# Two roundings moved behind attention steps, VectorE's w_out sums one down step later, six stores on ScalarE's queue

## The chip, the cores and the metric

One core of a Trainium2 chip runs the kernel. The metric is the device time of one execution in microseconds; of the kernel before there are three runs, 1019.55, 1022.45 and 1023.5, median 1022.45. Engines are called as the profile calls them: PE (TensorE; PEld its weight loads), DVE (VectorE), ACT (ScalarE), POOL (GpSimd), SP (SyncE, which here only issues DMAs).

## What is computed

A retention block, whose output is the input of a SwiGLU feed-forward block:

```python
scores = scale * np.matmul(q, k.transpose(0, 1, 3, 2))        # (8, 8, 576, 576), head_dim 64
Dmat = np.where(rel >= 0, gamma[:, None, None] ** rel, 0.0)   # rel = query position - key position
attn = np.matmul(scores * Dmat, v)
x = attn.transpose(0, 2, 1, 3).reshape(4608, 512)
g, val = x @ w_gate, x @ w_val                                # 512 -> 1536
out = (g * (1.0 / (1.0 + np.exp(-g))) * val) @ w_out          # 1536 -> 512
```

## The kernel before

**Attention.** Each of the 8 batches has 4 pairs of heads; pair i is one unit of work. `tick(t)` (L737) is attention step t: it finishes pair t-2, multiplies pair t-1 and prepares pair t, so that three pairs are in flight. On PE a step is own values (L532), new states (L543), earlier values (L555, L559) and scores (L567, L573). Around them ACT copies the even states (L584), scales the keys (`keys`, L507) and the queries (L489), and copies outputs into x (L626, L656); DVE masks the scores (L580, L590), sums states (L596 to L608) and transposes queries and keys of the next pair (L492). `load(i)` (L254) issues a pair's loads on SP: four for q and four for k of 128-byte rows, one each for k and v as rows.

**Feed-forward.** The 4608 tokens are cut into tiles: one of 512, then four of 1024. Tile 0 is multiplied plainly: `up0(f)` (L842) makes the gate and value products of hidden block f, f = 0 to 11, into two of the four PSUM banks; ACT takes the silu (L856), DVE multiplies by it (L857). Then `down0(f)` (L862) multiplies the twelve hidden blocks by w_out in the order of `down_order` (8, 9, 1, 3, 10, 4, 6, 11, 5, 7, 0, 2), each into all four banks, so the first down step needs the banks of the last up step back. The later tiles use a fast matrix multiplication, with sums of x blocks, weight blocks and hidden blocks as operands (`up_stage`, `down_step`, L1042, L1186, L1381).

**Rounding of weights.** Weights arrive as raw float32 in 18 pieces (`order`), each of two halves, 36 halves j. For half j, `split(j)` takes it apart on ACT (L389, L390) and `rounding(j)` puts it together on DVE (L406, L407) and then calls `split(j + 1)`. The last piece, m = 17, is the last sixth of w_out; its halves are j = 34, needed by `down0(10)`, and j = 35, needed by `down0(11)`. In the kernel before, the plan of the up steps calls both just ahead of the last one, `up0(11)`.

**Sums of w_out.** The later tiles need sums of w_out blocks, 26 operands that are stored to DRAM (`dn_ops`). `out_sums(last)` (L919) makes them in nine groups of up to three operands: `groups` are the sums of the first two thirds of w_out on POOL, `last_groups` those of the last third on DVE. Sums are L879, L881 and L886; each operand's store (L956) is issued on SP as soon as the group is written down, so SP's queue meets the stores in the order of the program and waits at each for its sum. The sums rotate through a few places in SBUF (seven for POOL): a place is free again when its store has landed. `negate` (L915, L917) writes two negated blocks on ACT that POOL's sums read.

**The order around the change** is written out by hand; each engine executes its instructions in the order of the program. The up steps 2 to 11 of tile 0 come from a list, `plan`, that mixes `up0`, roundings, loads and steps 4 to 9 (`tick_at`); step 9 follows `up0(11)`. Then the loop over the twelve down steps (counted from 0) runs `down0`, step 10, 11, 12 and 13 after down steps 1, 3, 6 and 8, and after each down step one group of DVE's sums and one of POOL's. `go_on(n)` issues the next n pieces of an attention step that are still held back. After down step 9, `early_sums` starts the sums of x and of the up weights for tile 1 on DVE and POOL (L1042).

DMAs of SP and ACT count on eight semaphores, taken in turn as the build lays them out; an instruction that issues a DMA waits until the one that had its semaphore before has landed.

Of the kernel before, what the change touches and what calls it, by code (L numbers as in the profile page):

```python
# [131 lines left out]
def kernel(  # L132
# [32 lines left out]
    nc = tc.nc  # L165
# [15 lines left out]
    NQ = NF // 4  # L181
# [54 lines left out]
    def needed(n):  # L236

        last = (min(starts[n] + TW, NT) - 1) // S
        return last * HP + HP - 1 + 3
# [112 lines left out]
    order = [0, 1, 2, 3, 4, 5, 6, 12, 7, 8, 13, 9, 10, 14, 11, 15, 16, 17]  # L352
# [27 lines left out]
    def split(j):  # L380

        i, f = halves[j]
        bits = bits_of(i, f)
        top, ulp = [rest[:, part_at + 512 * (2 * n + j % 2) : part_at + 512 * (2 * n + j % 2 + 1)] for n in range(2)]
        blocks = lambda a: a.rearrange("p (c m) -> p c m", m=P)
        nc.scalar.activation(out=blocks(top), in_=bits[:, :, :, 1].bitcast(F32), func=AF.Prelu, scale=2.0 ** -112, alpha=2.0 ** 32)  # L389
        nc.scalar.activation(out=blocks(ulp.bitcast(I32)), in_=bits[:, :, :, 0].bitcast(U32), func=AF.Copy, scale=2.0 ** -29)  # L390
        parts[j] = top.bitcast(I32), ulp.bitcast(I32)
        m = j - 2 if 1 < j < 4 else j // 2
        if f and m != RAWS and m + RAWS + (m < RAWS) < len(order):
            if j == 3:
                held.append(lambda: load_w(m + RAWS + (m < RAWS)))
            else:
                load_w(m + RAWS + (m < RAWS))

    def rounding(j, ahead=True):

        i, f = halves[j]
        dst = weights[i][1][f].bitcast(I32)
        top, ulp = parts.pop(j)
        nc.vector.tensor_scalar(out=dst, in0=top, scalar1=3, scalar2=None, op0=ALU.logical_shift_left)  # L406
        nc.vector.tensor_tensor(out=dst, in0=dst, in1=ulp, op=ALU.add)  # L407
        if ahead and j + 1 < len(halves):
            split(j + 1)
# [289 lines left out]
    ends = [(n, x, hl) for n in range(2) for x in range(2) for hl in range(2)]  # L699
# [28 lines left out]
    pieces = []  # L728
# [95 lines left out]
    def go_on(n):  # L824
        for _ in range(min(n, len(pieces))):
            while part_on():
                pass

    def part_on():

        if pieces and isinstance(pieces[0], list):
            pieces[0].pop(0)()
            if pieces[0]:
                return True
            pieces.pop(0)
        elif pieces:
            pieces.pop(0)()
        return False
# [23 lines left out]
    def down0(f):  # L862
        for i, bank in enumerate(banks):
            nc.tensor.matmul(bank, hid0[f][:, ts(i, P)], w_dn[:, f // 4, f % 4].rearrange("p d x -> p (d x)"),
                             start=(f == down_order[0]), stop=(f == down_order[-1]))
# [10 lines left out]
    def add(eng, op, view, to=None):  # L876
        dst, srcs = view(int(op[1])) if to is None else to, [view(int(a)) for a in op[2:]]
        if op[0] == "neg":
            eng.tensor_scalar(out=dst, in0=srcs[0], scalar1=-1.0, scalar2=None, op0=ALU.mult)  # L879
        elif op[0] == "nad" and eng is nc.vector:  # L880
            eng.scalar_tensor_tensor(out=dst, in0=srcs[0], scalar=-1.0, in1=srcs[1], op0=ALU.mult, op1=ALU.subtract)  # L881
        elif op[0] == "nad":
            eng.tensor_tensor(out=dst, in0=srcs[0], in1=srcs[1], op=ALU.add)
            eng.tensor_scalar(out=dst, in0=dst, scalar1=-1.0, scalar2=None, op0=ALU.mult)
        else:
            eng.tensor_tensor(out=dst, in0=srcs[0], in1=srcs[1], op=ALU.add if op[0] == "add" else ALU.subtract)  # L886

    up_sets = [[dr.tile([P, 1792], F32, name=f"up{qd}_{o}") for o in SETS] for qd in range(NQ)]
    dn_ops = [dr.tile([P, 768], F32, name=f"dn{i}") for i in range(N)]
# [9 lines left out]
    def events_of(text):  # L899
        r = []  # L900
        for line in text:
            i, s = line.split("|")
            slot, ops = s.split(":")
            r += [(int(op[1]), op) for op in terms(ops)] + [(None, int(slot), int(i))]
        return r
# [10 lines left out]
        for n, s in enumerate((3, 5)):  # L916
            nc.scalar.mul(out=negatives[n], in_=w_dn[:, 0:2, s // 2, s % 2], mul=-1.0)  # L917

    def out_sums(last):  # L919


        place = {}

        def free(p):
            if not any(p is q for q in x0_places):
                sum_places.append(p)

        qs = NQ - 1 if last else slice(0, NQ - 1)
        eng, sum_places = (nc.vector, vector_places) if last else (nc.gpsimd, pool_places)
        events = events_of(OUT_SUMS if last else signed)  # L930

        def view(s):
            if s > 13:
                return negatives[s - 14]
            return w_dn[:, qs, s // 2, s % 2] if s < 8 else place[s]

        def used(e):
            return [e[1]] if e[0] is None else [int(a) for a in e[1][2:]]

        def release(k):  # L940

            for s in list(place):
                for e in events[k + 1 :]:
                    if s in used(e):
                        break
                    if s == e[0]:
                        free(place.pop(s))
                        break
                else:
                    free(place.pop(s))  # L950

        def do(k):
            e = events[k]
            if e[0] is None:
                _, slot, i = e
                nc.sync.dma_start(out=dn_ops[i].rearrange("p (q x) -> p q x", q=NQ)[:, qs], in_=view(slot))  # L956
            else:
                new = sum_places.pop(0)
                add(eng, e[1], view, new)
                if e[0] in place:  # L960
                    free(place[e[0]])
                place[e[0]] = new
            release(k)

        r, ends = [], [k for k, e in enumerate(events) if e[0] is None]
        for g in range(0, N, 3):
            lo, hi = ends[g - 1] + 1 if g else 0, ends[min(g + 2, N - 1)] + 1

            def group(lo=lo, hi=hi):
                for k in range(lo, hi):  # L970
                    do(k)

            r.append(group)
        return r
# [151 lines left out]
    def early_sums():  # L1126

        x_outer, x_inner, *_ = x_sets(1)
        _, _, w_outer, w_inner, store = w_sets(0)
        p = [w_inner(2) + store(2, True), w_outer(5), x_inner(2, nc.gpsimd), w_outer(6), w_inner(6) + store(6, True), x_inner(6, nc.gpsimd)]  # L1130
        v = [f for o in (5, 6, 3, 7) for f in x_outer(o, nc.vector)]
        return p, v
# [309 lines left out]
    def next_load(t):  # L1442
        if t + AHEAD < NP:
            load(t + AHEAD)

    groups, last_groups = out_sums(False), out_sums(True)
    todo = [m for m in range(3, len(order))]
    plan = []

    def round_until(i):  # L1450
        while todo and order.index(i) >= todo[0]:
            m = todo.pop(0)
            plan.extend(lambda j=j: rounding(j) for j in (2 * m, 2 * m + 1))
# [2 lines left out]
    plan.insert(1, lambda: tick(HP, HP, FIRST))  # L1456
    tick_at = {2: 4, 3: 5, 5: 6, 7: 7, 10: 8, 11: 9}
    for f in range(2, NF):
        round_until({4: 12, 6: 13, 8: 14, 9: 15, 10: 16, 11: 17}.get(f, f + 2))
        if f + 1 == NF:  # L1460
            plan.append(lambda: pool_places.extend(wide_places))
            plan.append(negate)
        plan.append(lambda f=f: up0(f, range(HP)))
        if f - 1 in tick_at and f < 7:
            plan.append(lambda t=tick_at[f - 1]: next_load(t))
        if f in tick_at and f > 2:
            plan.append(lambda t=tick_at[f]: tick(t, HP, FIRST))
            if tick_at[f] == HP + 1:
                plan.append(end_transposes)
        if f in (7, 10):  # L1470
            if f == 10:
                plan.append(lambda: next_load(9))
            plan.append(lambda t=tick_at[f]: next_load(t))
    assert not todo
    for f in plan:
        f()
    tick_at = {1: 10, 3: 11, 6: 12, 8: 13}
    for m, f in enumerate(down_order):
        down0(f)
        go_on(6)  # L1480
        if m in tick_at:
            tick(tick_at[m], HP, FIRST, tick_at[m] + 1 < needed(1))
            go_on(2)
        if last_groups:
            last_groups.pop(0)()
        if groups:
            groups.pop(0)()
        if m == 9:
            early, early_x = early_sums()
            go_on(len(pieces))  # L1490
        if m >= 9:
            for f in early_x[:4]:
                f()
            del early_x[:4]
            for f in [f for fs in early[:2] for f in fs]:
                f()
            del early[:2]
# [62 lines left out]
```

## Time and profile before

| what | value |
|---|---|
| median of 3 runs | 1022.45 us |
| profiled execution: time | 1022.88 us |
| profiled execution: span | 1021.2 us |
| granted PE clock, mean | 0.998 |
| PE busy | 1003.4 us (98%) |
| DVE busy | 718.9 us (70%) |
| POOL busy | 555.6 us (54%) |
| ACT busy | 286.2 us (28%) |

The attention of the first pairs and the loading of weights fill the first 60 us. Tile 0's up steps end at about 119 us, its down steps at 176 us; tile 1 runs to about 400 us, and the rest is shared by the other three. Times in the views count from the start of the span. A timeline row has the start, the time it covers, engine, line, operation, the tile written and the tile read, the shape and a count; in square brackets, how long the engine was idle before it and what released it. In a row of waits there are the total, the count and the longest. The table of stretches has the busy time of PE, PEld, DVE, ACT and POOL, the granted clock, the DMA engines' busy share and GB/s. Engine names that end in q are the engine's own queue, which issues DMAs.

### The profile page before, as it was taken

Reading aid. Unit: us, or ns where it says so; the run is one execution under the profiler, and the core shown is the slowest. Engines: PE = TensorE matmul, PEld = TensorE weight load, DVE = VectorE, ACT = ScalarE, POOL = GpSimd, SP = SyncE. Lnnn points to the kernel's source line nnn. Section 1 sums busy time; section 2 is a strip of 40 time slices with the busy share of each in tenths; the row PEclk is TensorE's granted clock in tenths of the full one; section 3 lists DMA queues with packets and bytes.
Section 4 is the critical chain, followed back from the end, with each engine's and each line's share of the span. In section 5 each row is a group of like instructions: output and inputs, shape, how many; then the busy total and the mean of one; then the engine's idle time right before and its main releaser. Section 6 shows DMA issues by size and latency. Waiting matters only on the chain.

```text
span 1021.2 us, 21316 instructions
## 1 busy us (share of the span) xinstructions
PE 1003.4 (98%) x8336; PEld 823.2 (81%) x8336; DVE 718.9 (70%) x1215; ACT 286.2 (28%) x636; POOL 555.6 (54%) x579
## 2 busy tenths in 40 slices
PE   6999999999999999999999999999999999999998
PEld 5645455888888888888888888888888888888887
DVE  5478889678787766876688678848575767566644
ACT  4466522132423312133332101233320012232110
POOL 3400348979572218575565248756672586566515
PEclk9999999999999999999999999999999999999999
DMA  9999877777496888746658776434454454445652
GB/s 239 256 273 258 198 213 257 204 232 207 124 262 162 247 205 229 200 158 189 188 167 226 191 187 202 166 127 148 168 179 148 146 194 145 144 156 179 186 158 96
DMA packets 278892, 194.38 MB, mean 190 GB/s; under 512 B 212552, under 2 KB 246088, under 8 KB 278792
## 3 DMA queue, kind: packets, MB, share of 16 engines
q1 hardware_dynamic: 251464, 94.70, 36.4%
q10 hardware_dynamic: 26688, 97.92, 29.0%
q8 instruction: 66, 1.08, 0.5%
q0 software_dynamic: 640, 0.39, 0.2%
q14 instruction: 34, 0.28, 0.1%
HBM read 154.04 MB, written 38.93 MB: 189 GB/s over the span
## 4 chain that ended last, share of the span: by engine, by line
PE 86%; DMA 5%; DVE 4%; ACT 2%; issue 1%; SPq 1%; POOL 0%; ACTq 0%; DVEq 0%
PE bankC L1186 11%; PE bankB L1186 11%; PE bankA L1186 11%; PE bankE L1186 11%; PE bankB L1381 7%; PE bankE L1381 7%; PE bankC L1381 7%; PE bankA L1381 6%; PE outer L1186 2%; PE inner L1186 2%; PE outer L532 2%; DMA rest<-in_moe_w_out_dram 2%; PE inner L573 1%; PE inner L543 1%; PE outer L559 1%
## 5 line engine op out<-in xcount | busy, mean ns | idle before, releaser
L1042 POOL TENSOR_TENSOR rest<-rest 128x512 f32<-128x512 f32 (+1 forms) x141 | 150.5, 1079 | 156.2 <-DVE rest L1042 114.1
L1201 POOL TENSOR_TENSOR arena<-rest,io 128x256 f32<-128x256 f32 x156 | 114.6, 746 | 82.7 <-ACT io L1200 82.3
L1200 ACT ACTIVATE io<-rest 128x256 f32<-128x256 f32 x192 | 79.3, 417 | 208.4 <-DVE rest L1042 146.1
L1186 PE MATMUL bankB<-rest,arena 128*128 128x256 f32 x448 | 114.9, 381 | 0.2
L1042 DVE TENSOR_TENSOR rest<-bankB,rest 128x512 f32<-128x512 f32 x116 | 78.3, 683 | 48.4 <-PE bankB L1186 33.8
L1186 PE MATMUL bankC<-rest,arena 128*128 128x256 f32 x416 | 106.3, 380 | 0.2
L1186 PE MATMUL bankA<-rest,arena 128*128 128x256 f32 x412 | 105.3, 380 | 0.6 <-DVE rest L1042 0.4
L1042 DVE TENSOR_TENSOR rest<-bankA,rest 128x512 f32<-128x512 f32 x110 | 74.3, 683 | 39.9 <-PE bankA L1186 19.7
L1042 DVE TENSOR_TENSOR rest<-bankC,rest 128x512 f32<-128x512 f32 x110 | 74.6, 684 | 33.7 <-PE bankC L1186 18.0
L1186 PE MATMUL bankE<-rest,arena 128*128 128x256 f32 x372 | 95.0, 381 | 0.4 <-DVE rest L1042 0.3
L1186 PEld LDWEIGHTS bankB<-rest,arena 128*128 128x128 f32 x448 | 84.5, 190 | 13.0 <-DVE rest L1042 1.5
L1042 DVE TENSOR_TENSOR rest<-bankE,rest 128x512 f32<-128x512 f32 x106 | 71.7, 684 | 30.3 <-PE bankE L1186 12.6
L1186 PEld LDWEIGHTS bankC<-rest,arena 128*128 128x128 f32 x416 | 78.3, 190 | 12.2 <-DVE rest L1042 1.0
L1186 PEld LDWEIGHTS bankA<-rest,arena 128*128 128x128 f32 x412 | 77.9, 190 | 12.3 <-DVE rest L1042 1.8
L1186 PEld LDWEIGHTS bankE<-rest,arena 128*128 128x128 f32 x372 | 69.8, 190 | 11.9 <-DVE rest L1042 1.8
L1042 POOL TENSOR_TENSOR arena<-arena 128x256 f32<-128x256 f32 (+1 forms) x76 | 70.9, 957 | 8.5 <-DMA up<-arena 4.8
L886 POOL TENSOR_TENSOR rest<-rest 128x512 f32<-128x512 f32 x21 | 29.1, 1407 | 77.8 <-DVE rest L407 59.3
L1381 PE MATMUL bankB<-arena 128*128 128x256 f32 x264 | 61.0, 381 | 0.0
L1381 PE MATMUL bankE<-arena 128*128 128x256 f32 x264 | 60.8, 380 | 0.0
L886 POOL TENSOR_TENSOR arena<-arena 128x768 f32<-128x768 f32 x24 | 47.1, 1964 | 15.5 <-DVE arena L1201 14.9
L1381 PEld LDWEIGHTS bankE<-arena 128*128 128x128 f32 x264 | 50.0, 190 | 6.9
L1381 PEld LDWEIGHTS bankB<-arena 128*128 128x128 f32 x264 | 49.8, 190 | 6.9
(267 smaller groups left out, 1891.6 us busy)
## 6 DMA issues: line engine op xcount, KB each, us to landing
arena<-up ACTq DMA_DIRECT2D x63, 896.0 KB, 4.6
arena<-dn ACTq DMA_DIRECT2D x65, 384.0 KB, 3.7
arena<-dn SPq DMA_DIRECT2D x39, 384.0 KB, 3.2
out_dram<-rest SPq DMA_DIRECT2D x31, 256.0 KB, 3.0
qk<-in_q_dram SPq DMA_DIRECT2D x108, 72.0 KB, 3.6
qk<-in_k_dram SPq DMA_DIRECT2D x108, 72.0 KB, 4.0
dn<-rest SPq DMA_DIRECT2D x26, 256.0 KB, 3.2
up<-arena SPq DMA_DIRECT2D x13, 512.0 KB, 4.0
```

The costliest lines, as they stand in the source:

```text
L532: m = nc.tensor.matmul(value(i, hl, c), s["v"][rows, at], ret[rows, c % 2 if whole(i) else hl, c // 2], start=start, stop=start, skip_grou ...
L543: nc.tensor.matmul(z[half[hl], r, c], s["kn"][chunk(i, hl, 2 * c + r)], s["v"][rows, at], start=True, stop=True, skip_group_check=True)
L559: nc.tensor.matmul(xr[half[hl]] if c + 1 == NC else value(i, hl, c), state[half[hl], c, :], s["qT"][half[hl], ts(c, L)], start=False, stop ...
L573: nc.tensor.matmul(sc[chunk(i, hl, 2 * c + r)[0], r if whole(i) else hl, c], kT[half[hl], at], qT[half[hl], at], start=True, stop=True, sk ...
L886: eng.tensor_tensor(out=dst, in0=srcs[0], in1=srcs[1], op=ALU.add if op[0] == "add" else ALU.subtract)
L1042: eng.tensor_tensor(out=out, in0=a, in1=b, op=ALU.add if sign > 0 else ALU.subtract)
L1186: m = nc.tensor.matmul(b[:, g * TB : (g + 1) * TB], w[:, g], x, start=(opens and g == 0), stop=True, skip_group_check=True)
L1200: nc.scalar.activation(out=s, in_=src[:, 0:TB], func=AF.Silu)
L1201: (nc.vector if busy and o != 2 else nc.gpsimd).tensor_tensor(out=hid[:, qd, 2 * H + h, 2 * T + t], in0=src[:, TB : 2 * TB], in1=s, op=ALU ...
L1381: nc.tensor.matmul(b[:, m * TB : (m + 1) * TB], lhs[:, qd, ts(m, P)], w[:, qd], start=(opens and qd == 0 and m == 0), stop=(qd == NQ - 1), ...
```

## The change

The roundings of the last piece, j = 34 and j = 35, leave the plan ahead of `up0(11)`. Half 34 is rounded at the end of the plan, behind step 9; half 35 in down step 1, behind all pieces of step 10, which are now issued at once there. DVE's groups of w_out sums begin in down step 1 instead of 0. POOL's begin with two groups in down step 0 and go on with one in each. The first six stores of POOL's sums, those of its first two groups, are issued on ACT's queue instead of SP's.

```diff
-    def out_sums(last):
+    def out_sums(last, soon=0):
...
-                nc.sync.dma_start(out=dn_ops[i].rearrange("p (q x) -> p q x", q=NQ)[:, qs], in_=view(slot))
+                queue = nc.scalar if k in ends[:soon] else nc.sync
+                queue.dma_start(out=dn_ops[i].rearrange("p (q x) -> p q x", q=NQ)[:, qs], in_=view(slot))
...
-    groups, last_groups = out_sums(False), out_sums(True)
+    groups, last_groups = out_sums(False, 6), out_sums(True)
...
     for f in range(2, NF):
-        round_until({4: 12, 6: 13, 8: 14, 9: 15, 10: 16, 11: 17}.get(f, f + 2))
+        round_until({4: 12, 6: 13, 8: 14, 9: 15, 10: 16, 11: 16}.get(f, f + 2))
...
-    assert not todo
+    assert todo.pop() == len(order) - 1 and not todo
+    plan.append(lambda: rounding(2 * len(order) - 2))
     for f in plan:
         f()
...
             tick(tick_at[m], HP, FIRST, tick_at[m] + 1 < needed(1))
-            go_on(2)
-        if last_groups:
+            go_on(2 if m > 1 else len(pieces))
+        if m == 1:
+            rounding(2 * len(order) - 1)
+        if last_groups and m:
             last_groups.pop(0)()
-        if groups:
+        for _ in range(min(len(groups), 1 if m else 2)):
             groups.pop(0)()
```

## The prediction

> **What bounds the kernel now.** I read the page's busy shares first, then the waits of TensorE (PE), then timelines of the stretch that the change touches, 112 to 260 us.
>
> ```profile
> PE 1003.4 (98%) x8336; PEld 823.2 (81%) x8336; DVE 718.9 (70%) x1215; ACT 286.2 (28%) x636; POOL 555.6 (54%) x579
> ```
>
> PE is idle for 17.8 us of 1021.2: 7.7 in the first 20 us, which the change leaves alone, and after 60 us crumbs of 0.5 and less, but for one. The waits of PE between 112 and 260 us have one row:
>
> ```profile
> PE bankE L864 <- DVE arena L857: 1.9, 1, 1.9
> ```
>
> So the change can win there and nowhere else. VectorE's (DVE) timeline shows who made it late: the last two roundings (L406, L407) stand ahead of the product L857 that frees bankE. The table of stretches shows what followed: PEclk, the granted clock, is 0.62 in the 4.5 us after the stall and 1.00 elsewhere.
>
> ```profile
> 120.91 1.64 DVE L407 CUSTOM_DVE_ANT_0 rest<-rest 128x1024 uint16<-128x1024 uint16 x1
> 122.47 1.49 DVE L406 TENSOR_SCALAR rest<-rest 128x512 int32<-128x512 int32 x1
> 124.10 1.53 DVE L407 CUSTOM_DVE_ANT_0 rest<-rest 128x1024 uint16<-128x1024 uint16 x1
> 125.55 0.68 DVE L857 TENSOR_TENSOR arena<-bankE,io 128x512 f32<-128x512 f32 x1
> ```
>
> ```profile
> 124.40:126.30 1.90, 0.02 (x1) 0.02 (x1) 1.90 (x4) 0.00 (x0) 1.90 (x2) 1.00 0.96 210
> 126.30:130.80 4.50, 4.50 (x7) 1.94 (x8) 4.32 (x13) 0.00 (x0) 0.45 (x1) 0.62 0.88 156
> ```
>
> **The stall goes.** In the new order L857 follows step nine's key transpose, which ends at 120.51. Its silu (ACT L856) starts at 118.30 and moves earlier, since the last split leaves the place ahead of it. So L857 runs 120.5 to 121.2; PE wants bankE at 124.38. The margin of 3.2 us is the cover; the stall returns only if L857 slips by more. That removes 1.90 us of stall. The three pairs of products behind it took 1.42, 1.71 and 1.41 us where every other pair takes 0.86: 4.54 - 2.58 = 1.96 us of half clock. Together **3.86 us**. Check: from the first product of the step to the next attention step PE needs 10.93 us here (121.54 to 132.47) and 7.06 one step later (134.73 to 141.79); the difference is 3.87. Every later date of PE is its row less 3.86.
>
> [...]
>
> **The moved roundings.** Each is an L406 and an L407, 0.42 and 0.69 us alone (99.35 and 99.91), 1.42 to 1.6 beside POOL's sums. The first now follows step nine's transposes (ends about 126.7), where DVE waits until 131 for step ten's scores anyway: hidden, 1 to 3 us into a gap of 4. Its weight is due in down step 4 (counted from 0), near 140. The second follows step ten's transposes and is due in down step 7, near 153; the cover is some 12 us, but the w_out sums queue behind it.
>
> **ScalarE's six stores.** ACT's scaling of step nine ends at 123.82; the split moved there (two of 0.57) ends at 125.0. Six issues of 0.4 to 0.5 us follow (SP's rows of the same store: 0.39 to 0.46, one 1.03), to 128. The POOL sums they store are ready: started at 116.8, once L917 is 1.1 us earlier, five sums of 1.3 to 1.7 end at 124. ACT is next needed at 131.1 for step ten's copy (134.93 - 3.86), so the issues cost nothing there; the cover is 3 us.
>
> But they reach SP's queue. All these DMAs share eight semaphores, and the built program has SP's v load of pair 11 wait for the first store's landing, the q loads of pair 10 for the second, third and fourth, its k loads for the fifth and sixth. Before, SP ran unhindered:
>
> ```profile
> 124.08 0.58 SPq L287 DMA_DIRECT2D v<-in_v_dram x1
> 124.77 3.42 SPq L282 DMA_DIRECT2D qk<-in_q_dram x4
> 128.23 2.12 SPq L282 DMA_DIRECT2D qk<-in_k_dram x4
> 130.45 0.44 SPq L287 DMA_DIRECT2D kn<-in_k_dram x1
> 130.99 0.59 SPq L287 DMA_DIRECT2D v<-in_v_dram x1
> 132.86 3.39 SPq L956 DMA_DIRECT2D dn<-rest x6
> ```
>
> A store of this size lands 2.3 to 4.7 us after its issue. I take 2.7 (172.48 to 175.23 in the trace, with little beside it): v at 127.8 instead of 124.08, the q and k loads 128.4 to 132.8, kn at 132.9 instead of 130.45, landing 3.6 later (4.1 in the row of 123.54, which stood behind a load of q and k) at 136.5, v at 137.8. Step eleven on PE needs kn scaled and v by 138.2 (142.07 - 3.86) and the transposed keys by 139.5 (143.37 - 3.86). ACT scales kn (0.96) and qk (0.87), DVE transposes (1.43): 136.5 + 3.3 = 139.8. **A new wait of 0.3 us**; between 0, at a landing of 2.3, and 6, at 4.7 with kn as late as its first use allows (130.45 to 137.66).
>
> **DVE's sums, a step later.** Behind those transposes (139.8) stand the second rounding (1.1), the first two groups (seven ops, 2.4: POOL waits then), step ten's masks and states (2.75), to 146.05; four sums of about 1.2 beside POOL (147.38 to 150.96 had three in 3.58), the transposes of step eleven (to 151.7, wanted at 152.6), six more sums (7.2), and step eleven's masks and states, done at 161.6. PE wants those at 161.2: **0.4 us** (0 to 1.5). PE is then 3.86 - 0.3 - 0.4 = 3.16 ahead.
>
> **POOL sets how much of this stays.**
>
> ```profile
> 138.12 1.35 POOL L886 TENSOR_TENSOR rest<-rest 128x512 f32<-128x512 f32 x1 [11.36 <-DMA dn<-rest]
> ...
> 161.32 5.48 POOL L886 TENSOR_TENSOR rest<-rest 128x512 f32<-128x512 f32 x4 [3.25 <-DMA dn<-rest]
> 166.77 7.65 POOL L1042 TENSOR_TENSOR arena<-arena 128x256 f32<-128x256 f32 x6
> ...
> 176.64 1.17 POOL L1042 TENSOR_TENSOR x_odd<-x_odd 128x256 f32<-128x256 f32 x1
> ```
>
> ```profile
> 217.66 0.72 POOL L1042 TENSOR_TENSOR rest<-arena 128x256 f32<-128x256 f32 x1 [5.26 <-DMA up<-rest]
> ```
>
> From 161.32 POOL never rests until 212.4, and SP's stores follow it; the landing of one starts the stretch at 217.66. Its sum that ends at 237.97 is read by a PE product at 238.38: **a margin of 0.41 us**. So PE may be ahead by 0.41 plus what POOL is ahead.
>
> POOL's 23 w_out sums: the eighth starts at 127.8 instead of 138.12, the thirteenth waits for a store that SP issues behind DVE's first group (143.4, landing 146.2; before, 147.89), then eleven run without a rest (1.42 each) to 161.9 instead of 166.77. Eight further sums later, at 171.7, POOL meets the in-place one of 176.64, which must wait for DVE's fifth x sum. DVE has seven w_out sums left at 161.6 (8.4 beside POOL, to 170.0), one x sum of 1.2, then four of 0.7 with POOL waiting: 174.1. POOL is 2.5 ahead there and loses 0.6 beside DVE's last three (1.17 for 0.73 a sum). POOL ahead: **1.9 us** (5 at most, if DVE were free; -1 if the keys of step eleven come at 142). PE may keep 0.41 + 1.9 = **2.3 us**.
>
> [...] In the trace the first of these sums ended at 119.23 to 120.6 and its store was issued at 134.28, behind loads and a DVE store on SP; that queueing is what goes. [...]
>
> **Sum.** The built programs are in the same order from about 205 us on, and PE waits there at most 0.5 us at a time, so what is left is kept. Profiled execution: 1022.88 (span 1021.2 and 1.7 around it) - 2.3 = 1020.6. The median of the runs, 1022.45, lies 0.4 below that execution: **1020.2 us**.
>
> **Rivals.**
> 1. Nothing new waits and POOL's margin is wider than I read it: all of 3.86 stays, 1018.6. For it: the stores may land in 2.3 us. Against: the 0.41. Chance 0.20.
> 2. Slower: SP's loads behind ACT's stores. If a store takes 4.7 us (156.49 to 161.19), kn of pair 10 is issued near 135, lands at 139 to 142, and the keys are ready at 142.3 to 145.4: 2.8 to 5.9 us of wait, and a wait over 1.9 brings the half clock (1.96) again: 0.9 to 4.0 more than is saved, 1023.4 to 1026.5. It decides when the keys come after 141.4 (139.5 + 3.86 - 1.96). For it: the DMA share is 0.88 at 126 to 131 us. Chance 0.18.
> 3. The half clock is not the stall's doing and stays: 1.90 saved; PE is then late enough for the new waits to vanish: 1020.6. Chance 0.07.
> 4. The new queue does not bring POOL forward, or DVE's later sums hold it: PE keeps the margin of 0.41 alone, 1022.0. Chance 0.15.
>
> The forecast, 1019.4 to 1021.2, has 0.40. The change does do what it says: the built order has six ACT stores and the moved roundings. The range 1018.0 to 1024.0 takes in all but the far half of rival 2 and the scatter of the runs (1019.55 to 1023.5). Half a per cent, about what a measurement can tell here, is 5.1 us: more than the 3.86 that there is to win, so faster by that has 0.04; slower by that needs the far end of rival 2, 0.05; same 0.91.
>
> **What would show it.** Right: no wait of PE on L857 and a clock of 1.00 at 124 to 131; ACT's six stores at 125 to 128; SP's loads of pair 10 some 3 us later; POOL's L1042 sums from about 162; a short PE wait on POOL near 236. Wrong: a PE wait of over 1 us in step eleven (L543 or L567), ACT's copy at 131 delayed by the stores, or the stretch of 217.66 no earlier.

## The result, and the profile after

The changed kernel takes 1023.78 us (median of 22 runs, 1020.77 to 1025.83), the kernel before beside it 1021.31 (22 runs, 1019.35 to 1024.71): a ratio of 1.0021, 95% interval 1.0013 to 1.0029. By the medians it is slower by about 2.5 us where the prediction had it faster by about 2. Its profiled execution took 1024.21 us, with a span of 1022.5.

The stall that the prediction started from is gone. Among the waits of PE in the changed kernel (total, count, longest; the rows left out between them belong to the first 25 us), these two fall in tile 0's down steps:

```profile
PE outer L532 <- ACT rest L626: 1.9, 1, 1.9
...
PE outer L567 <- DVE kT L492: 0.8, 1, 0.8
```

No row names L857 any more. In its place PE waits as long at L532, the own values of attention step thirteen (the loop's `tick(13)`), for ScalarE's L626. The stretches show both places; the columns are the busy times of PE, PEld, DVE, ACT and POOL, then the granted clock:

```profile
124.40:126.30 1.90, 1.90 (x6) 0.93 (x5) 1.83 (x6) 1.02 (x2) 0.80 (x1) 1.00 1.04 331
126.30:130.80 4.50, 4.50 (x136) 2.79 (x138) 3.66 (x4) 0.00 (x0) 3.82 (x4) 1.00 1.15 297
...
161.60:163.60 2.00, 0.11 (x5) 0.07 (x7) 1.86 (x8) 1.53 (x6) 2.00 (x4) 1.00 0.75 271
163.60:168.00 4.40, 4.31 (x72) 2.56 (x73) 4.37 (x5) 1.53 (x6) 4.30 (x5) 0.66 0.72 254
```

At 124.4 to 130.8, where the kernel before idled and then ran at a clock of 0.62, PE is busy at 1.00. At 161.6 it idles instead, and the clock of 0.66 follows there. The same two losses stand 37 us later. The wait on L567 comes on top. It is in step eleven, and costs more than its row says: from L532 at 138.12 to the next product of a down step at 141.75 the step took 3.63 us, where it takes 2.25 in the traces that have no wait there. VectorE's timeline ahead of that wait:

```profile
152.06 0.73 DVE L492 STREAM_TRANSPOSE kT<-rest 128x576 f32<-128x576 f32 x1
152.72 2.78 DVE L886 TENSOR_TENSOR rest<-rest 128x256 f32<-128x256 f32 x2
155.42 1.49 DVE L881 SCALAR_TENSOR_TENSOR rest<-rest 128x256 f32<-128x256 f32 x1
156.83 4.29 DVE L886 TENSOR_TENSOR rest<-rest 128x256 f32<-128x256 f32 x3
161.05 0.68 DVE L580 TENSOR_TENSOR ret<-inner,near 128x512 f32<-128x512 f32 x1
161.65 0.21 DVE L590 TENSOR_TENSOR ret_last<-outer,last_near 128x64 f32<-128x64 f32 x1
```

Six w_out sums, 8.3 us, stand between the transposes and the masks L580 and L590 of step twelve. ScalarE's timeline goes on from L590, and PE's row ends the chain:

```profile
161.89 0.21 ACT L656 COPY rest<-outer 128x64 f32<-128x64 f32 x1 [6.81 <-DVE ret_last L590]
162.00 0.92 ACT L626 COPY x_odd<-outer 128x256 f32<-128x256 f32 x3
162.94 0.53 ACT L626 COPY rest<-outer 64x128 f32<-64x128 f32 x2
```

```profile
163.53 0.29 PE L532 MATMUL outer<-ret,v 64*64 64x64 f32 x4 [1.89 <-ACT rest L626]
```

In the order of its program ScalarE's copies out of the PSUM tile `outer` follow L656, which waits for L590; PE writes `outer` again only when they are through, 1.6 us after L590. The six sums take 1.4 us each; GpSimd is at work beside them without a break (the first experiment shows what a sum takes without it):

```profile
149.87 12.38 POOL L886 TENSOR_TENSOR rest<-rest 128x512 f32<-128x512 f32 x9 [0.46 <-DMA dn<-rest]
```

### The profile page after: what moved, and what is told of

The parts are those of the page before. It is cut to its first block, busy times and chain, and to the rows that moved or that the text cites. A ratio compares the mean times of both kernels' runs of the same rounds, so it can differ in the third digit from the quotient of the medians.

```text
span 1022.5 us, 21316 instructions
## 1 busy us (share of the span) xinstructions
PE 1003.9 (98%) x8336; PEld 823.9 (81%) x8336; DVE 714.1 (70%) x1215; ACT 286.6 (28%) x636; POOL 551.4 (54%) x579
## 4 chain that ended last, share of the span: by engine, by line
PE 70%; DVE 2%; issue 0%; SPq 0%; DMA 0%; DVEq 0%; ACT 0%
PE bankC L1187 9%; PE bankB L1187 9%; PE bankA L1187 9%; PE bankE L1187 9%; PE bankB L1382 7%; PE bankE L1382 7%; PE bankC L1382 7%; PE bankA L1382 6%; PE inner L1187 2%; PE outer L1187 2%; DVE rest L1043 1%; PE outer L532 1%; PE outer L559 1%; PE inner L573 1%; PE inner L543 1%
## 5 line engine op out<-in xcount | busy, mean ns | idle before, releaser
L1043 POOL TENSOR_TENSOR rest<-rest 128x512 f32<-128x512 f32 (+1 forms) x141 | 150.5, 1078 | 156.7 <-DVE rest L1043 114.6
L1187 PE MATMUL bankB<-rest,arena 128*128 128x256 f32 x448 | 114.8, 381 | 0.1
L1043 DVE TENSOR_TENSOR rest<-bankB,rest 128x512 f32<-128x512 f32 x116 | 78.3, 683 | 46.7 <-PE bankB L1187 32.4
L1187 PE MATMUL bankC<-rest,arena 128*128 128x256 f32 x416 | 106.4, 380 | 0.3
L1187 PE MATMUL bankA<-rest,arena 128*128 128x256 f32 x412 | 105.3, 380 | 0.6 <-DVE rest L1043 0.4
L1043 DVE TENSOR_TENSOR rest<-bankA,rest 128x512 f32<-128x512 f32 x110 | 74.3, 683 | 45.0 <-PE bankA L1187 19.6
L1043 DVE TENSOR_TENSOR rest<-bankC,rest 128x512 f32<-128x512 f32 x110 | 74.5, 683 | 33.2 <-PE bankC L1187 17.4
L1187 PE MATMUL bankE<-rest,arena 128*128 128x256 f32 x372 | 95.0, 380 | 0.4 <-DVE rest L1043 0.3
L1187 PEld LDWEIGHTS bankB<-rest,arena 128*128 128x128 f32 x448 | 84.5, 190 | 12.6 <-DVE rest L1043 1.1
L1043 DVE TENSOR_TENSOR rest<-bankE,rest 128x512 f32<-128x512 f32 x106 | 71.6, 683 | 30.8 <-PE bankE L1187 15.4
L1187 PEld LDWEIGHTS bankC<-rest,arena 128*128 128x128 f32 x416 | 78.3, 190 | 12.5 <-DVE rest L1043 1.4
L1187 PEld LDWEIGHTS bankA<-rest,arena 128*128 128x128 f32 x412 | 77.9, 190 | 12.3 <-DVE rest L1043 1.8
L1187 PEld LDWEIGHTS bankE<-rest,arena 128*128 128x128 f32 x372 | 69.9, 190 | 11.7 <-DVE rest L1043 1.6
L1043 POOL TENSOR_TENSOR arena<-arena 128x256 f32<-128x256 f32 (+1 forms) x76 | 69.4, 937 | 11.2 <-DMA up<-arena 6.2
L1382 PE MATMUL bankA<-arena 128*128 128x256 f32 x240 | 55.3, 380 | 0.0
## 6 DMA issues: line engine op xcount, KB each, us to landing
rest<-in_moe_w_out_dram ACTq DMA_DIRECT2D x6, 1024.0 KB, 6.2
```

What stands on the lines that cost most here:

```text
L1043: eng.tensor_tensor(out=out, in0=a, in1=b, op=ALU.add if sign > 0 else ALU.subtract)
L1187: m = nc.tensor.matmul(b[:, g * TB : (g + 1) * TB], w[:, g], x, start=(opens and g == 0), stop=True, skip_group_check=True)
L1382: nc.tensor.matmul(b[:, m * TB : (m + 1) * TB], lhs[:, qd, ts(m, P)], w[:, qd], start=(opens and qd == 0 and m == 0), stop=(qd == NQ - 1), ...
```

## The experiments

The theories. **A**: the w_out sums of VectorE, a down step later, stand ahead of step twelve's masks and hold ScalarE's copies and so PE's step thirteen. **B**: SyncE's loads behind ScalarE's six stores. **C**: GpSimd's sums, with the margin of 0.41 us, bound any gain. **D** (added later): the stall on L857 costs little on average. Ratios are to the kernel before on the same chip. Diffs are against the changed kernel unless said.

**The roundings alone, e1_round_only.** Sums and stores as before.

```diff
-    groups, last_groups = out_sums(False, 6), out_sums(True)
+    groups, last_groups = out_sums(False), out_sums(True)
...
-        if last_groups and m:
+        if last_groups:
...
-        for _ in range(min(len(groups), 1 if m else 2)):
+        for _ in range(min(len(groups), 1)):
```

> Theory A (VectorE's w_out sums, a down step later, stand ahead of step twelve's masks; ScalarE's copies of outer wait for these masks and TensorE for the copies): with the sums back at their old down steps and the stores back on SP, only the roundings are moved; TensorE's wait in step thirteen (1.89 us) and the one in step eleven (0.83 us) are gone, and so is the one on L857. 1.9 to 3.9 us below the kernel before. Rival B (SP's loads behind ScalarE's stores are what costs): the same here, so it is told apart by the next three. Rival C (GpSimd's margin of 0.41 us near 238 us bounds any gain): at most 0.4 us below the kernel before, with a wait of TensorE on GpSimd in tile 1.

Measured 1021.11 us, 0.9996 (0.9988 to 1.0005): no loss, as A expected, but not the gain of 1.9 to 3.9 us that A expected with it. VectorE's sums show what GpSimd's company costs. The first row is from a stretch where GpSimd rested (126.4 to 136.7), the second from one where it worked through (143.3 to 163.8):

```profile
127.63 0.76 DVE L886 TENSOR_TENSOR rest<-rest 128x256 f32<-128x256 f32 x2
...
148.93 4.19 DVE L886 TENSOR_TENSOR rest<-rest 128x256 f32<-128x256 f32 x3
```

The same instruction takes 0.38 us alone and 1.40 beside GpSimd. The DMA engines do not explain it: they were busier in the stretch of the short sums (0.82 of the time) than in that of the long ones (0.55). In the kernel before it is the same: 0.94 in the stretch 141.4 to 142.8 with sums of 0.38 us, 0.33 in 147.4 to 151.0 with sums of 1.1.

**VectorE's sums from down step 0, e2_sums_early**, the rest as changed.

```diff
-        if last_groups and m:
+        if last_groups:
```

> The changed kernel with VectorE's sums beginning in down step 0 again. Theory A: five sums instead of six between step eleven's transposes and step twelve's masks, 1.4 us less there: the wait in step thirteen falls from 1.89 to about 0.5 us and the half clock behind it goes, 1.4 to 3.4 us below the changed kernel; the first sums may delay step ten's masks. Rival B: the wait in step eleven stays, less than 0.5 us below the changed kernel.

1021.74 us, 1.0004 (0.9993 to 1.0014); no wait on L626.

**All stores on SyncE, e3_stores_sp**, the rest as changed.

```diff
-    groups, last_groups = out_sums(False, 6), out_sums(True)
+    groups, last_groups = out_sums(False), out_sums(True)
```

> The changed kernel with the six stores on SP. Theory A: the wait in step thirteen stays above 1 us; step eleven's 0.83 us goes; 0 to 1 us below the changed kernel. Rival B: all of the loss goes, 2.5 us or more below the changed kernel.

1024.2 us, 1.0022 (1.001 to 1.0035), with the wait on L626 at 2.8 us. The loss stays without the six stores on ScalarE: as the cause of the loss B is refuted. Its wait is real all the same. Step eleven, 2.25 us in this trace, is longer by 1.2 to 1.7 us in six of the nine traces with the six stores on ScalarE, by 0.4 in one, and by nothing in two; it is longer in none of the six that have the roundings moved and all stores on SyncE. Here PE came to step thirteen without that delay and waited longer there, 2.8 us for 1.9, so the time did not show it.

**The sums kept away from step twelve, e4_sums_aside.**

```diff
-        if last_groups and m:
+        if last_groups and m not in (0, 4, 5):
```

> The changed kernel with no VectorE sums in down steps 4 and 5; the groups move to the steps behind step twelve's masks. Theory A: the wait in step thirteen and its half clock go, 1.9 to 3.9 us below the changed kernel, a little below the kernel before. Rival B: no more than 0.5 us below the changed kernel. Rival C: a wait of TensorE on GpSimd appears in tile 1 and takes part of it back.

1021.11 us, 1.0000 (0.9991 to 1.0009): the loss is gone. Nothing stands between the transposes and the masks now, and L626 is not waited for; step eleven still has B's wait, 1.6 us longer than without it:

```profile
152.77 0.73 DVE L492 STREAM_TRANSPOSE kT<-rest 128x576 f32<-128x576 f32 x1
155.75 0.69 DVE L580 TENSOR_TENSOR ret<-inner,near 128x512 f32<-128x512 f32 x1 [2.25 <-ACT even L584]
```

**Controls: e5_before_again, e17_before_third, e6_after_again and e18_after_third** are the two kernels unchanged.

> The kernel before, unchanged, once more: a second trace of it, and its time against itself. If the stall of 1.90 us of PE on VectorE's L857 and the window at half clock behind it belong to every execution, as the prediction took it, they stand in this trace too (1.9 us within 0.2, a window of about 3.4 us behind 124). If the window is chance, it is elsewhere or missing while the stall is there. The ratio should be 1 with an interval of about 0.001 to either side, which is the noise that all other ratios of this study are read against.

> The kernel before against itself once more. If 1.0014 was chance: within 0.001 of 1. If the comparison sets the kernel under study too high: 1.001 or more again. The stage from the first down step to tile 1 should take 52.2 to 52.5 us, or 54.2 with a window at half clock behind the stall.

> The changed kernel, unchanged, once more. Theory A (VectorE's six sums ahead of step twelve's masks, then ScalarE's copies out of outer, then PE's step thirteen) expects the wait of PE on L626 near 163 again, 1.5 to 3 us, and 1.0021 of before within 0.001. If the wait is missing in this trace while the ratio stays, A is not the cause.

> The changed kernel on the same chip: 1.002 to 1.003, by theory A 0.0015 to 0.003 above e17_before_third, with a wait of PE on L626 of 0.6 to 2.1 us, and the stage at 52 us, or 54 to 55.4 with a window at half clock.

The kernel before against itself came out at 1.0014 (1.0002 to 1.0025) and 1.0006 (0.9994 to 1.0017). So a single ratio nearer to 1 than about 0.0015 tells nothing here. The changed kernel came out at 1.0026 (1.0013 to 1.0038) and 1.0028 (1.0015 to 1.0041): the loss recurs. Its wait on L626 was 2.0 and 1.9 us, both times with the half clock behind it. Of the kernel before, e5_before_again has the stall on L857 without the half clock. Its row of waits, and its stretches, of which the second is the stall and the third the 4.5 us behind it, at 1.00 where the first execution had 0.62:

```profile
PE bankE L864 <- DVE arena L857: 1.7, 1, 1.7
```

```profile
127.70:129.40 1.70, 0.10 (x1) 0.00 (x0) 1.70 (x3) 0.00 (x0) 1.70 (x2) 1.00 0.82 171
129.40:133.90 4.50, 4.44 (x10) 1.82 (x10) 4.32 (x14) 0.00 (x0) 0.53 (x1) 1.00 1.00 176
```

The other, e17_before_third, has no stall at all. VectorE's and PE's timelines:

```profile
121.88 1.54 DVE L407 CUSTOM_DVE_ANT_0 rest<-rest 128x1024 uint16<-128x1024 uint16 x1
123.34 0.68 DVE L857 TENSOR_TENSOR arena<-bankE,io 128x512 f32<-128x512 f32 x1
```

```profile
125.06 1.02 PE L864 MATMUL bankE<-rest,arena 128*128 128x512 f32 x2
```

The last rounding and L857 stand 2.2 us earlier than in the first execution, so L857 ended at 124.0, before PE came to bankE.

**More sums: e7_sums_doubled and e9_more_sums.** The first was meant to double the sums ahead of the masks, and its expectation says so. It did not: the sums of down steps 4 and 5 both stood there already, and VectorE's order stayed as it was. So it is a further sample of the changed order, and the growth that its expectation names is not tested by it.

```diff
-        if last_groups and m:
-            last_groups.pop(0)()
+        for _ in range(min(len(last_groups), (0, 1, 1, 1, 0, 2)[m] if m < 6 else 1)):
+            last_groups.pop(0)()
```

> The changed kernel with VectorE's sums of down step 4 put behind those of down step 5, both ahead of step twelve's masks: the suspected cost about doubled, all else as it was. A: four more sums of 1.1 to 1.4 us stand ahead of ret_last (L590), so the wait of PE on L626 grows from 1.9 us by 4 to 6, and the time by as much, to 1028 to 1030 (ratio near 1.007). C (GpSimd's sums bound the rest): nothing of it, since GpSimd's work is untouched: 1024. If the time grows by less than 2 us, other work takes the place and A's price is not additive.

1024.49 us, 1.0031 (1.0015 to 1.0047), with a wait on L626 of only 0.6 us in its trace. The second moves the groups of steps 6 and 7 up to step 5, which makes 12 sums of 6:

```diff
+        for _ in range(min(len(last_groups), {0: 0, 5: 3, 6: 0, 7: 0}.get(m, 1))):
+            last_groups.pop(0)()
```

> The changed kernel with VectorE's sums of down steps 6 and 7 moved ahead to down step 5: six more of 128x256, 12 in place of 6 ahead of step twelve's masks (L580), as the order of VectorE's instructions shows; all else as it was. (The kernel e7_sums_doubled had moved step 4's to step 5, which leaves VectorE's order as it is; this one changes it.) A: six more sums at 0.4 us (GpSimd idle) to 1.4 us (GpSimd busy, as in the traces so far) are 2.4 to 8.4 us on L590, so the wait of PE on L626 grows from 1.9 us to between 4 and 9, and the time from 1023.8 to between 1026 and 1031. If VectorE's sums were not what PE waits for, nothing of it: 1024.

1032.19 us, 1.0103 (1.008 to 1.0126): slower than the changed kernel by 8, over the upper end of what A expected. The wait is within it, and the clock made the rest. VectorE's rows, the wait of PE, and the stretches, the second of them at a clock of 0.54:

```profile
158.12 4.29 DVE L886 TENSOR_TENSOR rest<-rest 128x256 f32<-128x256 f32 x3
162.34 1.48 DVE L881 SCALAR_TENSOR_TENSOR rest<-rest 128x256 f32<-128x256 f32 x1
163.74 4.92 DVE L886 TENSOR_TENSOR rest<-rest 128x256 f32<-128x256 f32 x5
168.59 0.68 DVE L580 TENSOR_TENSOR ret<-inner,near 128x512 f32<-128x512 f32 x1
```

```profile
PE outer L532 <- ACT rest L626: 8.2, 1, 8.2
```

```profile
160.00:166.30 6.30, 2.91 (x7) 0.95 (x5) 6.23 (x6) 0.00 (x0) 6.14 (x7) 1.00 0.65 227
166.30:177.50 11.20, 6.34 (x74) 3.89 (x75) 8.61 (x18) 3.06 (x12) 3.49 (x3) 0.54 0.79 276
```

No sums there (1.000), five with the stores on ScalarE (0.9998 to 1.0004), six (1.002 to 1.003), twelve (1.010): A holds for the loss. The gain that it promised without the sums did not come.

**The later sums alone, e10_sums_only**: the kernel before with this one part of the change.

```diff
-        if last_groups:
+        if last_groups and m:
```

> The kernel before with one part of the change alone: VectorE's sums from down step 1 in place of 0. A: L590 of step twelve comes as late as in the changed kernel, 161 to 162, but PE, which in the kernel before is later by its own stall on L857, needs the copies out of outer at 163.87: little or no wait on L626 (0 to 1 us), time 1021.3 to 1022.5, ratio 0.9995 to 1.0015. So the cost would come of both parts together. Rival: the later sums cost by themselves, whatever PE does (the stores behind them, GpSimd's and the later operands): 1023 to 1024, ratio 1.002.

1023.35 us, 1.0011 (0.9999 to 1.0023). The ratio is within A's expectation, is not told from 1 by the controls, and does not exclude the rival's 1.002 either. The trace decides more: it has the stall on L857 (1.6 us) and none on L626. The copies ended at 161.75 and PE, late by its own stall, wanted `outer` at 162.29.

**The stores with early sums: e8_early_sp** (e2_sums_early with all stores on SyncE), **then both once more on one chip, e11_early_again and e12_early_sp_again.**

```diff
-    groups, last_groups = out_sums(False, 6), out_sums(True)
+    groups, last_groups = out_sums(False), out_sums(True)
...
-        if last_groups and m:
+        if last_groups:
```

> The changed roundings and the changed kernel's two GpSimd groups at down step 0, but VectorE's sums from down step 0 and all stores on SyncE: e1_round_only with GpSimd a group ahead. In the trace of e1_round_only the 4.1 us that it was ahead of before at 170 shrank to 1.8 at three places, two of them waits for GpSimd's L1043 (near 200 and 230 of its span). C: with GpSimd a group earlier these two waits go, 4 us ahead at 170 and over 3 at 260, time 1018.5 to 1020.3, ratio 0.997 to 0.999. Against C: it gives the lead back as e1_round_only did, 1021. A and B expect no wait on L626 and none on L567 here.

> The kernel of e2_sums_early (changed roundings and stores, VectorE's sums from down step 0) unchanged, on the chip of e12_early_sp_again. If the 1.0004 of e2_sums_early and the 1.0033 of e8_early_sp were the chip's difference, both come out alike here. If the stores' queue makes it (with all stores on SyncE GpSimd's sums ran beside VectorE's six at 140, 1.2 us each in place of 0.37, and kT came 2 us late), this one is below 1.001 and e12_early_sp_again 0.002 above it.

> The kernel of e8_early_sp unchanged, on the chip of e11_early_again: 1.003 again and a wait of about 2 us of PE on kT (L492) near 155, if the sums of GpSimd and VectorE beside each other make it; within 0.001 of e11_early_again if it was the chip.

e8_early_sp: 1024.67 us, 1.0033 (1.0017 to 1.0048), and not the gain that C expected. The trace has a new wait, because GpSimd's sums now ran beside VectorE's six at 140, which took 1.2 us each (0.38 alone), and pushed the transposes back:

```profile
PE outer L567 <- DVE kT L492: 2.0, 1, 2.0
```

Side by side the two gave 1.0001 (0.9989 to 1.0014) for the stores on ScalarE and 1.0014 (0.9999 to 1.0028) on SyncE: the direction is the same, the intervals overlap. The second trace of the latter has no wait on kT but one of 1.4 us on L626, with five sums ahead of the masks: that wait is not tied to six. That the stores' queue matters with early sums is likely, not shown.

**Four sums of x taken off GpSimd: e13_round_relief, e14_before_relief, e15_early_relief, with e16_round_again as the baseline.** In `early_sums`, on e1_round_only, on the kernel before and on e2_sums_early:

```diff
-        p = [..., x_inner(2, nc.gpsimd), w_outer(6), ...]
+        p = [..., x_inner(2, nc.vector), w_outer(6), ...]
```

> The roundings moved alone (as e1_round_only), and four sums of x for tile 1 taken from GpSimd (171.15 to 175.7 in the trace of e1_round_only, some 4.5 us) to VectorE, which is idle there for 4.6 us: GpSimd comes some 4 us earlier into tile 1. C: the waits of PE for GpSimd's L1043 near 200 and 230 go, the lead stays, 1.5 to 2.5 us faster than e16_round_again, ratio to before 0.997 to 0.9985. D: no difference to e16_round_again, both 0.9995 to 1.0005.

> The kernel before with the same four sums on VectorE, nothing else. C: GpSimd limits before only in executions without the half clock, so it gains 0 to 1.5 us: ratio 0.9985 to 1.0. D: 1.0 within 0.0007. If the four sums on VectorE cost something in themselves (they stand ahead of the first evictions of tile 1), it is above 1.0005.

> The kernel of e2_sums_early with the same four sums on VectorE. Its own trace gave back only 0.2 of 3.0 us in tile 1, so C expects little: 0.9985 to 1.0003, and no better than e13_round_relief. D: as e2_sums_early, 1.0001 to 1.0004.

> The kernel of e1_round_only unchanged, as the baseline of e13_round_relief on the same chip: 0.9996 within 0.001, and a lead of PE at 170 that shrinks by 1 us or more up to 270.

0.9997 (0.9986 to 1.0008), 1.0002 (0.9988 to 1.0015), 0.9998 (0.9986 to 1.0009) and 1.0001 (0.9987 to 1.0015). The waits of PE for GpSimd's L1043 at 198 to 230, 0.2 and 0.3 us in e1_round_only and e4_sums_aside, are missing in these traces, in that of the baseline too, and the time is the same. Where C expected e13_round_relief 1.5 to 2.5 us faster than e16_round_again it was 0.2. The baseline's trace had no such wait to take away and no gain either, so C is not what takes the gain there.

No version beats the kernel before by more than the controls allow.

## Where the time came from

One stage holds it: from the first product of the first down step (L864) to the first product of tile 1 (L1186 before, L1187 after). In each profiled execution, worked out from PE's timeline:

| order | this stage, us | from tile 1's first product to PE's last, us |
|---|---|---|
| before (5 executions) | 54.2, 52.4, 52.2, 52.4, 50.4; mean 52.3 | mean 841.9 |
| changed (5, e3 and e7 among them) | 55.4, 54.1, 55.3, 55.0, 51.1; mean 54.2 | mean 841.6 |
| roundings alone (e1, e16, e13) | 50.4, 50.4, 50.4 | mean 842.7 |
| twelve sums (e9) | 62.9 | 841.3 |

(The row of before holds the kernel, e5, e10, e14 and e17; e10 differs in the sums and e14 in work of GpSimd and VectorE, and both keep the stall.) 50.4 us is what PE took in the four traces that have no wait in the stage. The kernel before adds 1.9 on average: a stall of 1.6 to 1.9 in four of five and the half clock behind one. So D is right by half: the stall with what follows it costs 1.9 us on average, not the 3.86 that the prediction counted, and not nothing. The changed order adds 3.8: the wait on L626 (0.6 to 2.8) in all five and the half clock behind four, together 3.3, and step eleven, longer by 1.4 and 1.2 us in two. So of the difference some 1.3 us is the wait on L626 with its half clock, less the stall of before, and 0.5 is step eleven. In the first two executions, 54.2 and 55.4, the stall with its half clock and the wait with its own nearly cancel (3.9 before, 3.6 changed), and step eleven's 1.4 is what is left. Behind the stage the changed order takes 0.3 less. The difference of 1.9 us lies beside what was measured: 2.3 to 2.9 us against the runs of the kernel before (1023.78, 1023.83 and 1023.97 against 1021.31, 1021.5 and 1021.11), and 1.1 and 2.1 against the two controls of it (1022.77 and 1021.87).

For the roundings alone the same account gives 1.9 less in this stage and 0.8 more behind it, a gain of 1.1; the comparisons show 0.0004 faster to 0.0001 slower, within what the controls leave open. Whether a gain of 0.1% is there, and what takes the 0.8, could not be settled. The orders without the late sums but with the six stores on ScalarE do not reach 50.4 in all traces either: 52.0 in e4_sums_aside, 51.7 in e11_early_again and 51.6 in e15_early_relief, by step eleven, and 50.8 in e2_sums_early.

## Why the prediction was wrong

**The failed step is "DVE's sums, a step later", 0.4 us (0 to 1.5).** It was 1.9 us plus the half clock (1.7). The path was right up to VectorE; three things in it were not.
- It took the masks and states as what PE waits for, and left out ScalarE's copies out of `outer`, 1.6 us behind L590. PE came at 161.64, and the masks alone (L580 ended at 161.73) would have held its first product by 0.1 us. In the kernel before, these copies ended some 3.2 us before PE wanted `outer` (rows below). That margin was in the profile and was not read. In the changed kernel PE came 2.2 us earlier and the copies ended 2.8 us later, together 1.8 us more than the margin: the wait.
- The six sums took 8.3 us, not 7.2: 1.4 each beside GpSimd.
- They began 1.0 us later than worked out, behind transposes that were themselves late. By these two the states were done at 163.84 and not at 161.6, so on the prediction's own path, too, the term was too small; no run separates how much of the wait that alone would have made.

ScalarE's last copy and PE's first product of step thirteen in the kernel before:

```profile
160.18 0.53 ACT L626 COPY rest<-outer 64x128 f32<-64x128 f32 x2
```

```profile
163.87 1.01 PE L532 MATMUL outer<-ret,v 64*64 64x64 f32 x32
```

**The stall goes**: right. L857 ended at 120.5 and bankE was free.

**The 1.96 us of half clock** was counted as a sure part of the saving. It followed the stall in one execution of the four that had one (two of them the kernel before as it is), so the profiled execution of before was not a typical one. The rival that doubted the half clock (0.07) was nearer to the mean for the stall. The prediction did give its slower rival the half clock again behind a wait over 1.9 us; a wait of that size then came at another place.

**ScalarE's stores and SyncE's loads**: the mechanism was there, the size was another. In the first trace SyncE's loads waited 0.9 us for the stores to land (L287 0.7, L282 0.2), and 2.1 for a load of k ahead of them; the kernel before has neither wait there. The k rows of pair 10 were issued at 133.52, for 130.45 before and 132.9 expected. The prediction had 0.3 us of wait; step eleven was longer by 1.4 us in the first trace, by nothing in the second, and by 1.2 in the third. The k rows, expected at 136.5, were there at 137.69:

```profile
137.69 0.96 ACT L507 ACTIVATE kn<-kn,tab 128x256 f32<-128x256 f32 x2 [3.60 <-DMA kn<-in_k_dram]
```

With the stores on SyncE (e3_stores_sp) this wait went and the loss was the same. In e4_sums_aside the wait stayed and the loss was gone. So the slower rival had the right sign and a wait that exists, but not the one that the loss goes with.

**GpSimd's margin of 0.41 us** never came to bear, since PE was late and not early; and where PE was early, taking work off GpSimd brought nothing. The cap of 2.3 us was the wrong place to look. The lead of GpSimd itself came out as worked out, 1.9 us (the stretch of 217.66 began at 215.73), but not by the new queue. With all stores on SyncE (e3_stores_sp) GpSimd's ninth sum did begin 8 us later (136.43 for 128.18), yet its x sums began at 161.98 for 162.22 and that stretch at 215.77. So the fourth rival's first half, that the new queue does not bring POOL forward, holds in this order of the sums. With VectorE's sums a step earlier it does not: the x sums began at 160.06 with the stores on ScalarE (e2_sums_early) and at 163.59 with them on SyncE (e8_early_sp).

**The range** (1018.0 to 1024.0) held the time by luck: losses that the forecast had too small or left out ate more than the saving. The sign was wrong.

## What to carry to other kernels

When an engine is moved forward, list every wait that has so far ended unseen before it and subtract: the smallest margin on the way, here the 3.2 us of ScalarE's copies behind VectorE's last mask, takes the gain. Here each engine passed a delay on through what stood next in its program (VectorE's six sums of 8.3 us became a wait of 1.89 us on PE, by way of ScalarE), so follow a later instruction to the reader of the buffer that it frees, across engines. Two waits in a row hid each other: with the earlier one gone (step eleven, 1.4 us) the later one was 2.8 us for 1.9 and the time as it was (e3_stores_sp, a ratio of 1.0022 for 1.0021), so read both in the trace before calling one of them harmless. Before counting a stall as a saving, see it in a second execution of the same kernel, and set the comparison beside the kernel against itself.

## What was not expected of the hardware

**The half clock does not follow from the length of the gap alone.** The 20 traces have 11 stretches at half clock (a granted clock of 0.50 from 127 to 130 in the kernel before and from 165 to 168 in the changed one) between the first 8 us and the last 10, ten of them some 3.4 us long and that of e9_more_sums some 10, each at or right behind a wait of PE of 1.59 us or more. All five waits of 2.35 us and more had one, six of the thirteen between 1.59 and 2.04 us had one, and none of the seven from 1.32 to 1.47 us. So 1.89 us was enough in the changed kernel, and 1.59 (a gap with no releaser shown) in e16_round_again, while 2.0 us had none behind it in e8_early_sp. What decides between them these traces do not show.

**VectorE beside GpSimd.** A sum of 128x256 takes 0.38 us of VectorE alone and 1.40 beside GpSimd's sums, a factor of 3.7; the rounding step L407 0.69 and 1.64 (at 99.91 and 120.91 in the kernel before).
